# Moving the skip product, the rotations and one row-size pass in the second block of an S5 and Mish kernel

## The chip, the cores and the metric

The kernel runs on one core of one Trainium2 chip. The metric is the time of one execution on the device in microseconds (us). Of the kernel before there are three timed executions and one execution under the profiler.

The five engines have queues of their own. In the profile PE is the engine of the matmuls, PEld its weight loads, DVE the vector engine, ACT the scalar engine, POOL is GpSimd, and SP starts most of the DMAs. Instructions on one engine run in the order of its queue. An instruction that needs something from another engine waits on a semaphore, and everything behind it in the same queue waits with it.

## The reference: what is computed

From x (2048 x 1024) two branches are computed on the normalised rows xn = layernorm(x), and both are added to x:

```
xn  = layernorm(x)
Bu  = xn @ B_bar^T                        # complex, 1024 states
h_t = Lam_bar * h_(t-1) + Bu_t            # over 2048 steps
y   = 2 Re(h @ C^T) + xn * Dskip          # S5 branch, with the skip product
act = mish(xn @ w1 + b1)                  # 3584 columns
out = x + y + act @ w2
```

The part that the change touches most is the skip product xn * Dskip and its addition to x.

## The kernel before, in words

**Blocks.** The 2048 rows are done in four blocks of 512 (`blk` 0 to 3). The change concerns the second one, `blk == FAST == 1`; where the change in words says "block 2", this one is meant. A block lies in four row tiles of 128 (`q` 0 to 3): `xx` holds x, `xn` the normalised rows, `xnT` their transpose. Each block has a stage that projects into the states and into the Mish columns, a stage that multiplies the Mish columns by w2 (`tail`, line 1421: 28 column tiles by 8 output units), and a last one that multiplies the states by C (also line 1421, with hT).

**The order written out by hand.** In the second block the input projections are made by a form of Strassen's product with seven smaller products. `project_fast` walks through the string `WHOLE`, one token after another, and puts what the token stands for at the end of the queues:

- `a` to `d` with a number from 1 to 7: one of the seven products of a pair of state tiles (pair 0 to 3). `product` (line 935) issues 8 matmuls on PE, 128x256 each; `evacuate` then takes the sum out of PSUM.
- `p q s w` with a number: the same for a quad of Mish columns (`w_product`, line 1007, and `w_evacuate`, lines 1027 and 1044).
- `r` with a number: `rotate_in` of a state tile, three DVE instructions (lines 897, 903 and 905).
- `j` with a number: the skip product of a row tile.
- `T`: an ACT scaling of a rotation table. `k0`: one pending step that makes weight sums on DVE (line 1157) and stores them from POOL's queue (line 1136). `P`: weight sums on DVE (line 1669). `v`: a scaling of raw weights.
- `u` with a number: the first six column tiles of one output unit of the next stage. `g`: a Mish on ACT. `l`: loads of the next block's x, and `n`: loads of raw w1, both from POOL's queue.

**What an evacuation does.** A product leaves its sum in one of three PSUM banks X, Y and Z of its pair or quad. After product 1 and product 5, and after 6, ACT copies the bank to one of four buffers (`snaps`, line 952 for the pairs). After 1 for the pairs (2 for the quads), after 3 and after 7 DVE adds a bank and a copy into the result: a join (line 960 for the pairs, line 1044 for the quads). The copy buffer and the bank come free when the join has run.

The banks are shared over time. Pair c has X, Y, Z = 4, 5, 6 and pair d has 0, 1, 2. Quad s has 7, 5, 6 and quad w has 3, 1, 2. So s5 writes bank 6, which the join after c3 has to free, w5 writes bank 2 (join after d3), and c4 writes bank 4 (join after c7).

**The skip product.** `skip_slow` (lines 601 to 606) does it on POOL for the second block: a product into `xn` in place, and an addition to `xx`. The other blocks use `ln_skip` (lines 592 to 600), which does the same two steps on DVE with `mt` for the product.

**The statistics of the next block.** After `project_fast`, `next_stats` (lines 575 to 579) makes sums of the next block's rows on ACT, and `w_abs(0)` (line 1092) sizes the raw weights of quad 0 on ACT, one pass over 128x4096. The loop over the eight state tiles follows: `recur` (lines 1383, 897, 1390, 1392) on DVE for each. At tile 1 `next_root` (ACT line 583, DVE lines 585 and 586) and `next_scale` (ACT, line 590) stand in it, then `w_abs(1)`, `w_abs(2)` and `w_row(1)`. What they size is used in `w_exponent(1)` after the last tile. The normalised rows of the next block go through `transpose_dma` in SP's queue.

**Loads.** SP fills a ring of seven slots (lines 444 and 447). The load of a slot stands behind a wait until PE has used up what was in it.

Of the kernel before, what the change touches and what calls it, by code (L numbers as in the profile page):

```python
# [5 lines left out]
ALU = mybir.AluOpType  # L6
# [157 lines left out]
def build_kernel(nc, A_x, A_Lambda_re, A_Lambda_im, A_B_re, A_B_im, A_C_re, A_C_im,  # L164
# [18 lines left out]
    SPLIT = range(2, NB)  # L183
    GROUPS = ((0, 7), (7, NPL), (NPL, NPL + 8), (NPL + 8, NF), (12, 16), (16, 20), (20, 24), (24, 28))
    TILES = [*range(12)]
    WHOLE = ("a2 a1 b2 b1 a5 b5 P4 P5 a6 b6 v6 P6 P7 a3 b3 P0 a7 b7 P1 j0 p1 q1 a4 b4 "
# [3 lines left out]
    STEPS = ("p1 p5 p2 q1 q5 k0 k0 p6 q2 s1 k0 p7 s5 p3 k0 q6 s2 k0 p4 q7 k0 q3 k0 s6 q4 k0 m3 k0 g0 a2 a1 k0 s7 s3 k0 b2 b1 k0 s4 g1 m2 l0 a5 "  # L190
            "b5 a6 b6 a3 b3 a7 b7 c2 d2 a4 b4 c5 c1 d5 d1 h12 r0 c6 c3 h13 d6 d3 h14 c7 h15 w1 d7 r1 w5 w2 c4 d4 w6 x1 x5 x2 k0 w7 k0 w3 r2 "
            "x6 w4 y1 y5 y2 k0 x7 k0 x3 y6 A0 x4 z1 z5 g2 h8 h9 h10 M1 z2 y7 y3 z6 B0 h11 y4 z3 z7 u0 u2 r7 u1 z4 u7 r3 g3 r4 r6 r5")
# [20 lines left out]
    def sb(name, shape, dtype):  # L213
# [25 lines left out]
    xx = sb("xx", [P, 2, NQ, D], bf16)  # L239
    b_xx = [[Buf("xx%d_%d" % (i, q), parts=[Buf("xx%d_%d_%d" % (i, q, h)) for h in range(2)])  # L240
             for q in range(NQ)] for i in range(2)]
    s_xx = [[DmaSem(nc, "d_xx%d_%d" % (i, q)) for q in range(NQ)] for i in range(2)]
    xn = sb("xn", [P, NQ, D], bf16)
# [3 lines left out]
    dsk = sb("dsk", [P, D], bf16)  # L247
    b_dsk = Buf("dsk")
# [344 lines left out]
    def ln_skip(blk, q):  # L593

        i = blk % 2
        m = mt[:, q % 2, :, :].rearrange("p a t -> p (a t)")
        vop(lambda e: e.tensor_tensor(m, xn[:, q, :], dsk[:], op=ALU.mult),
            reads=[b_xn[q], b_dsk], writes=[b_m[q % 2]])
        vop(lambda e: e.tensor_tensor(xx[:, i, q, :], xx[:, i, q, :], m, op=ALU.add),
            reads=[b_xx[i][q], b_m[q % 2]], writes=[b_xx[i][q]])  # L600

    def skip_slow(blk, q):
        xb, b_x = xx[:, blk % 2, q, :], b_xx[blk % 2][q]
        pop(lambda e: e.tensor_tensor(xn[:, q, :], xn[:, q, :], dsk[:], op=ALU.mult),
            reads=[b_xn[q], b_dsk], writes=[b_xn[q]])
        pop(lambda e: e.tensor_tensor(xb, xb, xn[:, q, :], op=ALU.add), reads=[b_x, b_xn[q]], writes=[b_x])

    def transpose_dma(q):
        SP.dma(lambda e: e.dma_start_transpose(xnT[:, :, q * P:(q + 1) * P], xn[:, q, :]),
# [464 lines left out]
    def w_load(i):  # L1074
        sem = DmaSem(nc, "d_wraw%d" % i, nper=4)
        for ci in range(2):
            for kh in range(2):
                dst, b_dst = w_unit(w_raw(i, ci, kh))
                f0 = (4 * i + 2 * ci) * P
                src = B_w1[kh * NH * P:(kh + 1) * NH * P, f0:f0 + 2 * P].rearrange("(k p) f -> p k f", p=P)  # L1080
                PO.dma(lambda e, dst=dst, src=src: e.dma_start(dst.rearrange("p (k f) -> p k f", k=NH), src),
                       sem, writes=b_dst)
# [6 lines left out]
    def w_abs(i):  # L1089
        kind, t = w_raw(i, 0, 0)  # L1090
        v, b_v = (hb, b_hbf) if kind == "h" else (act, b_actf)
        aop(lambda e: e.activation(CT[:, :, 1, TB:D], v[:, t:t + 8, :], AF.Abs, accum_out=wsm(0, i, i + 1)),
            reads=b_v[t:t + 8], writes=b_snap + [b_wsm[0][i]])
# [211 lines left out]
    def project_fast(blk, order, open_unit):  # L1305
        keep = {}
        for o in order.split():
            kind, n = o[0], int(o[1:])
            if kind == "r":
                rotate_in(n)  # L1310
            elif kind == "u":
                open_unit(n)
            elif kind == "G":
                act_scale(n)
            elif kind == "g":
                mish(blk, n)
            elif kind == "k":
                if steps or later:
                    some(1)
                    ring_fill()  # L1320
            elif kind == "e":
                if later:
                    later.pop(0)()
            elif kind in "mMht":
                {"m": d2_load, "h": d2_row, "t": act_sums, "M": lambda n: d2_load(n, AC)}[kind](n)
            elif kind in "AB":
                recur(blk, n, (kind,))
                done.append((blk, n))
            elif kind == "P":
                sums_B(3 - n // 4, (n % 4,))  # L1330
            elif kind == "f":
                scale_B(n)
            elif kind == "T":
                table_scale(n)
            elif kind == "j":
                skip_slow(blk, n)
            elif kind == "S":
                row_scales()
            elif kind == "I":
                for _ in range(n):  # L1340
                    item_done()
            elif kind == "l":
                for q in range(NQ):
                    load_x(PO, blk + 1, q)
            elif kind == "n":
                w_load(n)
            elif kind == "v":
                w_scale(n)
                w_sums(n, True)
            elif kind in QUADS:  # L1350
                w_product(blk, QUADS.index(kind), n)
                w_evacuate(blk, QUADS.index(kind), n, keep)
            else:
                product(blk, "abcd".index(kind), n)
                evacuate("abcd".index(kind), n, keep, kind in "ab" and blk != FAST)
        assert blk < NB - 1 or not (steps or later)
# [331 lines left out]
    for blk in range(NB):  # L1688
# [60 lines left out]
        if near and blk not in SPLIT:  # L1749
            for q in range(NQ):  # L1750
                next_stats(blk + 1, q)
            w_abs(0)
        if blk == NB - 1:
            next(out_stage)
        for j in range(NJ):
            if blk == 0 and j == NJ - 1:
                rows_scale(0)
                w_load(3)
                rows_fetch(0)
            if (blk, j) not in done:  # L1760
                recur(blk, j)
            if near and j == (4 if blk in SPLIT else 1):
                next_root()
                for q in range(NQ):
                    next_scale(blk + 1, q)
            if blk in SPLIT:
                if near and j == 0:
                    d2_scale(1)
                if near and j == 1:
                    next(out_stage)  # L1770
                    for g in range(4, 8):
                        row_sizes(blk, g)
                    next(out_stage)
                    d2_load(5)
                    some(4)
                    d2_load(0)
                    recur(blk, 2)
                    done.append((blk, 2))
                    row_powers(20, NF)
                    row_bound()  # L1780
                    d2_scale(5)
                    for q in range(NQ):
                        next_stats(blk + 1, q)
                if near and j == 2:
                    some(4)
                if near and j == 3:
                    recur(blk, 4, "A")
                    some(4)
                    recur(blk, 4, "B")
                    done.append((blk, 4))  # L1790
                    row_most()
                if near and j == 4:
                    for q in range(NQ):
                        transpose_dma(q)
                    d2_scale(0)
                if j == 6 and not near:
                    vop(lambda e: e.tensor_tensor(KS[:, 1, :, :], KS[:, 1, :, :], KS[:, 3, :, :], op=ALU.add),
                        reads=[b_KS[1], b_KS[3]], writes=[b_KS[1]])
                continue
            if blk:  # L1800
                if j == 1:
                    next(out_stage)
                    w_load(2)
                    w_abs(1)
                    w_abs(2)
                    w_row(1)
                if j == 7:
                    w_exponent(1)
                    row_powers(0, 20)
                    for i in (0, 1, 2):  # L1810
                        w_scale(i)
                continue
            if j == 0:
                ln_root()
                for q in range(NQ):
                    ln_scale(1, q)
                w_exponent(0)
            scale_C(j)
            if j:
                keep_C(j - 1)  # L1820
            if j < 4:
                next(out_stage)
            if j < 3:
                row_sizes(0, j + 7)
            if j == 3:
                for i in range(NHS):
                    rows_load(i)
            for i in {4: (0, 1, 2), 5: (3, 4, 5, 6), 6: (7, 8, 9, 10), 7: range(11, 16)}.get(j, ()):
                rows_size(i)
# [61 lines left out]
```

## Time and profile before

| what | us |
|---|---|
| median of three timed runs | 601.29 (600.86 to 601.71) |
| the profiled execution, its own time | 601.42 |
| its span, from the first to the last instruction | 600.2 |
| PE busy in the span | 588.9 |
| DVE, ACT, POOL busy | 500.1, 386.6, 179.3 |
| mean granted PE clock, as a share of full speed | 0.991 |

The span is 1.2 us shorter than the profiled execution's own time. The rows below are read so: "216.92 1.04 PE L1007 ... x8" is a row of the timeline, it begins 216.92 us after the span's start, lasts 1.04 us, is issued at line 1007 of the kernel and has eight instructions; a bracket behind it tells how long the engine was idle before it and whom it waited for. Matmul rows overlap, since a matmul's end lies behind the start of the next; the pace is read from start to start. In a row of the windows view, each engine's busy time stands in the order PE, PEld, DVE, ACT and POOL, then the granted PE clock, the busy share of the DMA engines, and GB/s.

### The profile page before, as it was taken

Reading aid. Unit: us, or ns where it says so; the run is one execution under the profiler, and the core shown is the slowest. Engines: PE = TensorE matmul, PEld = TensorE weight load, DVE = VectorE, ACT = ScalarE, POOL = GpSimd, SP = SyncE. Lnnn points to the kernel's source line nnn. Section 1 sums busy time; section 2 is a strip of 40 time slices with the busy share of each in tenths; the row PEclk is TensorE's granted clock in tenths of the full one; section 3 lists DMA queues with packets and bytes.
Section 4 is the critical chain, followed back from the end, with each engine's and each line's share of the span. In section 5 each row is a group of like instructions: output and inputs, shape, how many; then the busy total and the mean of one; then the engine's idle time right before and its main releaser. Section 6 shows DMA issues by size and latency. Waiting matters only on the chain.

```text
span 600.2 us, 9754 instructions
## 1 busy us (share of the span) xinstructions
PE 588.9 (98%) x3651; PEld 356.5 (59%) x3651; DVE 500.1 (83%) x722; ACT 386.6 (64%) x518; POOL 179.3 (30%) x233
## 2 busy tenths in 40 slices
PE   9999999999999959999999999999999999999998
PEld 7644444444448847544448888744445888854444
DVE  6998898999898898919956956999399578789996
ACT  4849985488588635896255656898450798893320
POOL 2899300223653690600121611135210023100000
PEclk9999999999999988999999999999999999999999
DMA  9999999996899565988698958999997966988831
GB/s 251 302 242 281 222 181 240 322 381 184 255 331 350 193 212 162 315 294 206 198 309 313 405 217 293 354 314 319 259 283 277 391 248 219 333 316 325 293 128 70
DMA packets 115993, 161.90 MB, mean 270 GB/s; under 512 B 56010, under 2 KB 67018, under 8 KB 115946
## 3 DMA queue, kind: packets, MB, share of 16 engines
q1 hardware_dynamic: 96768, 104.42, 57.9%
q0 software_dynamic: 14112, 46.28, 22.4%
q10 hardware_dynamic: 5066, 10.57, 4.8%
q8 instruction: 29, 0.48, 0.3%
q14 instruction: 18, 0.15, 0.1%
HBM read 115.09 MB, written 34.08 MB: 249 GB/s over the span
## 4 chain that ended last, share of the span: by engine, by line
PE 95%; DVE 2%; DMA 1%; issue 1%; ACT 1%; SPq 1%; DVEq 0%
PE ps L1421 42%; PE ps L1007 18%; PE ps L935 11%; PE ps L859 9%; PE ps L1478 7%; PE ps L1367 5%; DMA ring<-in_B_w_dram 1%; PE ps L678 1%; DVE mt L897 1%; PE ps L669 0%; DVE hT L905 0%; DVE hT L903 0%; DVE hT L960 0%; PE ps L1444 0%; ACT act L1027 0%
## 5 line engine op out<-in xcount | busy, mean ns | idle before, releaser
L1421 PE MATMUL ps<-ring,act 128*128 128x512 bf16 x672 | 145.9, 379 | 0.0
L1421 PEld LDWEIGHTS ps<-ring,act 128*128 128x128 bf16 x672 | 65.7, 98 | 78.4
L1027 ACT ACTIVATE snaps<-ps,par,cs 128x256 f32<-128x256 f32 x98 | 53.6, 563 | 59.0 <-PE ps L1007 42.7
L1421 PE MATMUL ps<-ring,hT 128*128 128x512 bf16 x370 | 80.3, 379 | 0.0
L1007 PE MATMUL ps<-TT,ring 128*128 128x256 f16 x576 | 72.1, 275 | 7.6 <-DVE hT L960 7.6
L897 DVE TENSOR_TENSOR mt<-hT,tab 128x2048 bf16<-128x2048 bf16 (+1 forms) x56 | 71.2, 1272 | 1.3
L1007 PEld LDWEIGHTS ps<-TT,ring 128*128 128x128 f16 (+1 forms) x576 | 56.5, 98 | 15.7 <-DVE hT L960 7.9
L1184 POOL DMA_DIRECT2D w2d<-hb x42 | 30.0, 715 | 117.1 <-DVE hb L1212 71.0
L1421 PEld LDWEIGHTS ps<-ring,hT 128*128 128x128 bf16 x370 | 36.2, 98 | 43.6
L1383 DVE TENSOR_TENSOR_SCAN hT<-cs,qi,hT 128x512 bf16<-128x512 f32 x48 | 58.9, 1267 | 0.0
L1044 DVE SCALAR_TENSOR_TENSOR act<-ps,cs,snaps 128x512 bf16<-128x512 f32 x54 | 39.9, 748 | 21.2 <-PE ps L1007 19.4
L859 PE MATMUL ps<-xnT,ring 128*128 128x512 bf16 x264 | 57.3, 379 | 0.0
L1007 PE MATMUL ps<-xnT,ring 128*128 128x256 bf16 x432 | 54.6, 273 | 0.0
L1007 PEld LDWEIGHTS ps<-xnT,ring 128*128 128x128 bf16 (+1 forms) x432 | 42.4, 98 | 5.5
L859 PEld LDWEIGHTS ps<-xnT,ring 128*128 128x128 bf16 x264 | 25.8, 98 | 30.9
L882 ACT ACTIVATE act<-act 128x2048 bf16<-128x2048 bf16 (+3 forms) x12 | 32.8, 2756 | 6.8 <-DVE act L1030 6.8
L1136 POOL DMA_DIRECT2D wsd<-hb x35 | 19.0, 544 | 58.9 <-DVE hb L1157 31.0
L960 DVE TENSOR_TENSOR hT<-ps,snaps 128x512 f16<-128x512 f32 x36 | 23.9, 686 | 12.8 <-ACT snaps L952 10.4
L1142 ACT ACTIVATE hb<-hb,cs 128x2048 bf16<-128x2048 bf16 x10 | 19.4, 1994 | 22.4 <-DVE cs L1131 15.9
L867 ACT ACTIVATE act<-ps,par 128x512 bf16<-128x512 f32 (+1 forms) x40 | 23.9, 655 | 10.6 <-PE ps L859 10.5
L1367 PE MATMUL ps<-xnT,BT 128*128 128x512 bf16 x128 | 27.8, 379 | 0.0
L1421 PE MATMUL ps<-CT,hT 128*128 128x512 bf16 x128 | 27.8, 379 | 0.0
(226 smaller groups left out, 1014.4 us busy)
## 6 DMA issues: line engine op xcount, KB each, us to landing
ring<-wsd SPq DMA_DIRECT2D x126, 256.0 KB, 5.4
ring<-in_B_w_dram SPq DMA_DIRECT2D x62, 512.0 KB, 5.7
ring<-ctd SPq DMA_DIRECT2D x24, 512.0 KB, 4.4
ring<-w2d SPq DMA_DIRECT2D x24, 512.0 KB, 5.2
w2d<-hb POOLq DMA_DIRECT2D x42, 256.0 KB, 5.2
wsd<-hb POOLq DMA_DIRECT2D x35, 256.0 KB, 5.0
hb<-in_B_w_dram POOLq DMA_DIRECT2D x20, 256.0 KB, 5.9
ctd<-CT ACTq DMA_DIRECT2D x8, 512.0 KB, 5.8
```

The source lines that it names most:

```text
L859: PE.mm(lambda e, k=k, w=w: e.matmul(ps[:, bank, :], lhsT=w, rhs=xnT[:, k, :], start=k == 0, stop=k == NK - 1), reads=[b_ring[s]] + b_xnT, ...
L882: aop(lambda e: e.activation(t, t, AF.Mish), reads=b, writes=b)
L897: vop(lambda e: e.tensor_tensor(mt[:], u.unsqueeze(1).to_broadcast([P, 2, 2, TB]), tab[:, :, j, :].unsqueeze(2).to_broadcast([P, 2, 2, TB] ...
L935: PE.mm(lambda e, w=w, x=x, o=o, begin=begin, end=end: e.matmul(ps[:, bank, o:o + TH], lhsT=w, rhs=x, start=opens and begin, stop=end, ski ...
L1007: PE.mm(lambda e, w=w, x=x, o=o, begin=begin, end=end: e.matmul(ps[:, bank, o:o + TH], lhsT=w, rhs=x, start=opens and begin, stop=end, ski ...
L1027: aop(lambda e, o=o, p=p, j=j: e.activation(o, p, AF.Identity, scale=ig, bias=b1(f0 + j)), reads=[b_ps[b], b_par, b_ig], writes=b_dst)
L1044: vop(lambda e: e.scalar_tensor_tensor(out=dst, in0=bank(b), scalar=ig, in1=src, op0=ALU.mult, op1=ALU.add), reads=[b_ps[b], b_snap[k], b_ ...
L1184: PO.dma(lambda e: e.dma_start(w2d[at // 4][:, at % 4 * TB:(at % 4 + 2) * TB].rearrange("p (j t) -> p j t", j=2), t[:, :, d, :]), sem, rea ...
L1367: PE.mm(lambda e, j=j, ci=ci, k=k, bank=bank: e.matmul(ps[:, bank + ci, :], lhsT=BT[:, ci, j, k, :], rhs=xnT[:, k, :], start=k == 0, stop= ...
L1383: vop(lambda e, ci=ci, init=init: e.tensor_tensor_scan(out=hT[:, ci, j, :], data0=cj("r", j).to_broadcast([P, TB]), data1=hT[:, ci, j, :], ...
L1421: PE.mm(lambda e: e.matmul(ps[:, u, :], lhsT=lhsT, rhs=rhs, start=st_, stop=last, skip_group_check=blk == NB - 1), reads=reads, writes=[b_ ...
L1478: PE.mm(lambda e: e.matmul(ps[:, bank, :], lhsT=lhsT, rhs=rhs, start=st_, stop=end, skip_group_check=True), reads=[b_t, b_ring[s]], writes ...
```

## The change

Three things are changed, all in the second block:

1. `j0` to `j3` call `ln_skip` (DVE) and no longer `skip_slow` (POOL), which goes away. `j0` moves from a place before p1 to one behind d1, `j1` and `j2` from before c1 and before c5 to one behind T6, `j3` from before c7 to one behind d7.
2. All eight rotations move back in the order. Before, r0 stood behind d1, r1 behind T6 and r2 behind d7. Now r0 stands behind d4, r1 behind w2, r2 behind w7, r3 behind w4, and r4 to r7 in the last pieces. The order of the products is the same.
3. `w_abs(0)` moves from behind `next_stats` to behind `next_scale` and `w_load(2)`.

```diff
-    WHOLE = ("a2 a1 b2 b1 a5 b5 P4 P5 a6 b6 v6 P6 P7 a3 b3 P0 a7 b7 P1 j0 p1 q1 a4 b4 "
+    WHOLE = ("a2 a1 b2 b1 a5 b5 P4 P5 a6 b6 v6 P6 P7 a3 b3 P0 a7 b7 P1 p1 q1 a4 b4 "
              "k0 k0 p5 q5 k0 p2 q2 k0 p6 q6 P2 T4 p3 P3 q3 p7 q7 k0 c2 d2 p4 q4 T5 "
-             "k0 k0 k0 j1 c1 d1 r0 j2 c5 d5 T6 r1 c6 d6 T7 c3 d3 j3 c7 d7 r2 s1 s5 c4 d4 "
-             "r3 w1 w5 s2 w2 s6 w6 r4 s3 w3 s7 w7 u4 s4 w4 r5 u5 l0 u6 u7 n0 g4 g5 n1 r6 g6 g7 r7")
+             "k0 k0 k0 c1 d1 j0 c5 d5 T6 j1 j2 c6 d6 T7 c3 d3 c7 d7 j3 s1 s5 c4 d4 r0 "
+             "w1 w5 s2 w2 r1 s6 w6 s3 w3 s7 w7 r2 u4 s4 w4 r3 u5 l0 u6 u7 n0 g4 r4 g5 n1 r5 g6 r6 g7 r7")
...
-    def skip_slow(blk, q):
-        xb, b_x = xx[:, blk % 2, q, :], b_xx[blk % 2][q]
-        pop(lambda e: e.tensor_tensor(xn[:, q, :], xn[:, q, :], dsk[:], op=ALU.mult),
-            reads=[b_xn[q], b_dsk], writes=[b_xn[q]])
-        pop(lambda e: e.tensor_tensor(xb, xb, xn[:, q, :], op=ALU.add), reads=[b_x, b_xn[q]], writes=[b_x])
...
             elif kind == "j":
-                skip_slow(blk, n)
+                ln_skip(blk, n)
...
                 next_stats(blk + 1, q)
-            w_abs(0)
...
                     w_load(2)
+                    w_abs(0)
                     w_abs(1)
                     w_abs(2)
                     w_row(1)
```

## The prediction

> **What bounds the kernel now.** I read the page's busy shares first, then the table of who waited for whom, then the windows and the timeline where it pointed.
>
> ```profile
> PE 588.9 (98%) x3651; PEld 356.5 (59%) x3651; DVE 500.1 (83%) x722; ACT 386.6 (64%) x518; POOL 179.3 (30%) x233
> PE ps L1007 <- DVE hT L960: 7.6, 1, 7.6
> ```
>
> PE is busy nearly throughout, so the kernel gets faster only where PE stands still or runs slowly. In the table of waits one wait of PE is longer than 1.0 us: a single one of 7.6 us for a join of DVE (L960). The windows show where, and what it costs beyond itself (PE's busy time is the third number, the granted clock stands after the bracketed counts).
>
> ```profile
> 215.00:220.00 5.00, 2.96 (x28) 2.41 (x25) 4.96 (x3) 0.77 (x1) 4.86 (x3) 1.00 0.90 328
> 220.00:225.00 5.00, 0.00 (x0) 0.00 (x0) 4.97 (x4) 0.00 (x0) 4.17 (x2) 0.57 0.01 2
> 225.00:230.00 5.00, 4.41 (x21) 3.15 (x22) 4.93 (x8) 2.84 (x5) 0.00 (x0) 0.50 0.27 72
> ```
>
> From 220 to 225 PE does nothing while DVE and POOL are full, and from 225 to 230 PE works at a granted clock of 0.50. PE's timeline gives the price.
>
> ```profile
> 216.92 1.04 PE L1007 MATMUL ps<-xnT,ring 128*128 128x256 bf16 x8
> 225.59 1.89 PE L1007 MATMUL ps<-TT,ring 128*128 128x256 f16 x8 [7.63 <-DVE hT L960]
> ...
> 230.68 1.15 PE L1007 MATMUL ps<-xnT,ring 128*128 128x256 bf16 x8
> 231.67 1.04 PE L1007 MATMUL ps<-TT,ring 128*128 128x256 f16 x8
> 232.54 1.91 PE L1007 MATMUL ps<-xnT,ring 128*128 128x256 bf16 x16
> ```
>
> In the order of the tokens the first row is s1, the second s5, then c4 and d4, then w1 (230.68), w5 (231.67) and s2. At full clock a product takes 0.87 us, from 231.67 to 232.54. From the start of s1 to that of w5 lie five products, 4.37 us at 0.874 each; they took 231.67 - 216.92 = 14.75 us. **The stop costs 10.38 us**: 7.63 of waiting, 24 matmuls in 5.09 us instead of 2.62 (2.47), and 0.28 at the edges.
>
> Why the join is late is seen where DVE and POOL stand side by side.
>
> ```profile
> 205.57 2.86 DVE L1157 TENSOR_TENSOR hb<-hb 128x1024 f16<-128x1024 bf16 x4
> 211.35 1.29 DVE L960 TENSOR_TENSOR hT<-ps,snaps 128x512 f16<-128x512 f32 x2 [2.92 <-ACT snaps L952]
> 212.56 2.21 DVE L897 TENSOR_TENSOR mt<-hT,tab 128x2048 bf16<-128x2048 f16 x1
> 214.80 2.22 DVE L903 TENSOR_TENSOR hT<-mt 128x512 bf16<-128x512 bf16 x1
> 216.95 2.34 DVE L905 TENSOR_TENSOR hT<-mt 128x512 bf16<-128x512 bf16 x1
> 219.32 3.02 DVE L897 TENSOR_TENSOR mt<-hT,tab 128x2048 bf16<-128x2048 f16 x1
> 222.38 2.22 DVE L903 TENSOR_TENSOR hT<-mt 128x512 bf16<-128x512 bf16 x1
> ...
> 224.85 2.47 DVE L960 TENSOR_TENSOR hT<-ps,snaps 128x512 f16<-128x512 f32 x4
> 227.25 1.21 DVE L897 TENSOR_TENSOR mt<-hT,tab 128x2048 bf16<-128x2048 f16 x1
> ...
> 229.29 1.23 DVE L897 TENSOR_TENSOR mt<-hT,tab 128x2048 bf16<-128x2048 f16 x1
> ...
> 246.43 2.46 DVE L1383 TENSOR_TENSOR_SCAN hT<-cs,qi,hT 128x512 bf16<-128x512 f32 x2
> ```
>
> ```profile
> 208.72 0.54 POOL L1136 DMA_DIRECT2D wsd<-hb  x1 [0.18 <-issue]
> 209.28 2.14 POOL L604 TENSOR_TENSOR xn<-xn,dsk 128x1024 bf16<-128x1024 bf16 x1
> ...
> 213.64 3.11 POOL L604 TENSOR_TENSOR xn<-xn,dsk 128x1024 bf16<-128x1024 bf16 x1
> 216.89 2.12 POOL L606 TENSOR_TENSOR xx<-xx,xn 128x1024 bf16<-128x1024 bf16 x1
> ...
> 221.41 2.91 POOL L606 TENSOR_TENSOR xx<-xx,xn 128x1024 bf16<-128x1024 bf16 x1
> ```
>
> Behind the joins of c1 and d1 come r0 and r1, and only then the joins of c3, d3, c7 and d7 (the four at 224.85). A rotation takes 2.04 us when POOL is quiet, from 227.25 to 229.29 (r2). r0 and r1 ran while POOL multiplied and added, and took 212.56 to 224.85 = 12.29 us, 8.2 more than two quiet ones. Their ends follow POOL's: POOL's rows end at 216.75, 219.01 and 224.32, and the next DVE instruction ends at 217.02, 219.29 and just before 224.85. So each DVE instruction with two SBUF operands waits for a POOL instruction. s5 needs the bank that the join of c3 frees. That join ended at 224.85 + 0.69, and PE went on at 225.59.
>
> **The change part by part.**
>
> *Skip products on DVE.* POOL loses eight instructions, and nothing on POOL then computes in this stretch; its last DMA issue before it is at 208.72. DVE gains eight. Their price is to be seen in the third block's rows, and a locked one in the first block, beside POOL.
>
> ```profile
> 297.45 0.69 DVE L597 TENSOR_TENSOR mt<-xn,dsk 128x1024 bf16<-128x1024 bf16 x1
> ...
> 303.05 0.68 DVE L1676 TENSOR_TENSOR TT<-xnT 128x1024 f16<-128x1024 bf16 x1
> ```
>
> ```profile
> 29.69 1.76 DVE L597 TENSOR_TENSOR mt<-xn,dsk 128x1024 bf16<-128x1024 bf16 x1
> 31.48 1.06 DVE L599 TENSOR_TENSOR xx<-xx,mt 128x1024 bf16<-128x1024 bf16 x1
> ```
>
> Four skips run from 297.45 to 303.05, so an instruction takes 5.60 / 8 = 0.70 us. The locked pair averages 1.41. I take 0.70: the locked pair ran beside computing POOL rows, which are gone here, and beside POOL's DMA issues the four DVE instructions at 205.57 took 0.72 each. Below 0.70 nothing speaks for a gain.
>
> *The order on DVE.* The joins of c1 and d1 waited for ACT's copies (the bracket at 211.35), and what ACT and PE do before is unchanged, so DVE is free at 212.56 as before. Then j0, j1, j2: 6 x 0.70 = 4.20, to 216.76. The four joins took 224.85 to 227.25, 0.60 each: c3 ends at 217.36, d3 at 217.96, c7 at 218.56, d7 at 219.16, each 0.09 later counting the last one's full 0.69. PE would like to start s5 at 216.92 + 0.87 = 217.79 (bank freed at 217.45: no wait), c4 at 218.67 (218.65: just in time), d4 at 219.54 (219.25). With the 0.05 from a join's end to PE (225.54 to 225.59), c4 waits some 0.03. So the 10.38 us go, all but 0.1 at most; each 0.1 us by which a skip instruction is longer adds 0.6 behind it.
>
> What is late next? j3 takes 219.16 to 220.56. Behind it r0 stands where r3 stood and r1 about where r4 stood, at 2.04 each, so the joins of s and w have no more ahead of them than before, when PE did not wait for them. r2 comes behind the join of w7, and r3 to r7 when only the open units are left to PE. With PE's rows moved 10.38 earlier, w7's join ends near 230.0, and six rotations last until 242.3. The first `recur` began at 246.43 before, so even DVE's long chain starts 4 us earlier.
>
> *The size pass behind the scaling.* It costs no work, only order.
>
> ```profile
> 261.52 1.28 ACT L1092 ACT_TABLE_LOAD   x1
> 262.81 3.62 ACT L1092 ACTIVATE CT<-hb 128x4096 bf16<-128x4096 bf16 x1
> 268.17 0.18 DVE L585 RECIPROCAL ln<-ln 128x4 f32<-128x4 f32 x1 [12.80 <-ACT ln L583]
> 306.33 0.17 DVE L1408 TENSOR_TENSOR qi<-qi,qt 128x8 f32<-128x8 f32 x1
> 317.25 1.04 PE L1007 MATMUL ps<-xnT,ring 128*128 128x256 bf16 x8
> ```
>
> DVE waited 12.80 us for the root, behind a pass of 1.28 + 3.62 + 0.19 = 5.1 us on ACT. The pass goes behind `next_scale`, so the wait shrinks to some 2 us (DVE's wait began at 255.37 and begins 4 earlier, at 251.2; ACT's statistics end 10.4 earlier than 261.52, at 251.1, and a table load of 1.28 and the root follow). DVE goes on near 253 and no longer at 268.17, so its last work before the third block would end near 306.3 - 15 = 291, and PE's block near 317.25 - 10.4 = 306.9. Before, the cover was 317.25 - 306.33 = 10.9 us, after it some 15. This edit is worth nothing in the time, since PE and not DVE sets the end; without the cover it would be a gain of up to 12.80 - 2 = 10.8 us, not a loss. `w_row(1)` isn't delayed, since ACT does the same work before the third pass ends.
>
> *The queues.* The skips issue no DMA, and POOL's waits are shorter, not longer. SP's ring waits for PE, so its loads move with PE.
>
> ```profile
> 201.44 14.17 SPq L444 DMA_DIRECT2D ring<-wsd  x13
> 232.78 2.11 SPq L447 DMA_DIRECT2D ring<-in_B_w_dram  x2
> DMA to landing us min/median/max: 3.3/5.1/5.3
> 239.53 1.46 PE L1421 MATMUL ps<-ring,act 128*128 128x512 bf16 x6
> ```
>
> The thirteen loads of s and w weights were issued by 201.44 + 14.17 = 215.6. With the 5.3 of the w2 loads taken for them too, an estimate, the last has landed by 221; PE wants w1, which is early among them, at 220.4 and the last, s4, at 230.4. The third w2 load goes out at 234.5, lands 5.3 later at the longest (the third row is for five of these loads), at 239.8, and is wanted at 239.53 + 0.87 = 240.4. All three move with PE, so 0.6 us of margin stay.
>
> **Sum.** 601.42 - 10.38 + 0.05 = 591.09 for the profiled execution. That execution stands 0.13 above the median of the runs, less than their spread, so I give **591.1 us**.
>
> [...]
>
> **The rivals.**
>
> *A shorter stop stays.* Some joins still come late, by a skip instruction that is longer than 0.70, or by a copy of ACT that a join needs. For it: c4 has no slack. Against it: no row of a quiet POOL shows more than 0.72. At 0.80 the stop is 0.6 us. In the trace the half clock came some 2.8 us after PE's stop at 217.96 (the windows' 0.57 between 220 and 225), so a stop below that costs itself alone: 591.8 to 593.9.
>
> *The time saved is lost downstream.* PE comes 10.4 us earlier to the third w2 load, which is late: the pause no longer lets the DMA engines empty (busy share 0.01 between 220 and 225). For it: 0.6 us of margin. Against it: the load is bound to PE, and to lose all it has to take 5.3 + 0.6 + 10.4 = 16 us against a longest of 5.3. Then 601, no change; half of it gives 596.
>
> [...]
>
> **How the numbers follow.** Forecast (590.4 to 591.8): 0.80. Shorter stop (591.8 to 593.9): 0.10. Lost downstream: 0.07, of which 0.03 end within 0.2% of before and 0.04 near 596. Slower: 0.03. The range goes from 590.4 (the sum less 0.56, by which the fastest run lies under the profiled execution, rounded down) to 593.9, the end of the first rival; it holds 0.9 of the cases before any doubt about them. About 0.2% (1.2 us) can be told from no change here: faster 0.94, same 0.03, slower 0.03.
>
> **What would show it.** In the table of waits PE's 7.6 us for L960 is gone; no window of the second block has a PE clock below 0.9; PE goes from s1 to w5 in 4.4 us; lines 597 and 599 show four more instructions each near 0.69; the rotations all take 2.0; DVE's wait at L585 is near 2 us. I am wrong if skip rows near 215 last over 1 us, if PE waits for DVE before c4, or if PE stops at the first open unit (239.53 before, 229.15 after) for a load.

## The result, and the profile after

The changed kernel takes 591.11 us (median of five runs, 590.79 to 591.26), against 601.29 us before (five runs, 600.86 to 601.71). The ratio is 0.983, with a 95% interval of 0.9816 to 0.9844. The forecast was 591.1. The profiled execution took 591.11 us, with a span of 589.9 us.

The change takes out six lines ahead of the places of interest, so line numbers fall by 6: the joins of the pairs are at L954 (L960 before), the rotations at L891, L897 and L899, the products at L929 and L1001.

PE's first line on the page and its whole table of waits are now these (the table's columns: who waited for whom, total us, times, longest us):

```profile
PE 586.5 (99%) x3651; PEld 355.8 (60%) x3651; DVE 494.2 (84%) x730; ACT 384.6 (65%) x517; POOL 159.9 (27%) x225
PE ps L625 <- DVE filler L457: 1.0, 1, 1.0
PE ps L663 <- DMA ring<-in_B_w_dram: 0.2, 1, 0.2
```

The wait of 7.6 us is gone, and what is left lies in the first 12 us of the span. The windows of the same stretch as before:

```profile
215.00:220.00 5.00, 5.00 (x49) 4.48 (x47) 4.93 (x9) 2.69 (x5) 0.00 (x0) 1.00 0.94 337
220.00:225.00 5.00, 5.00 (x49) 4.48 (x46) 3.96 (x7) 3.45 (x7) 0.54 (x1) 1.00 0.57 193
225.00:230.00 5.00, 5.00 (x45) 4.21 (x43) 4.60 (x7) 2.15 (x4) 0.82 (x2) 1.00 0.97 341
```

PE is busy for all 15 us, at a clock of 1.00, beside a DVE that is nearly as full as before. The timeline shows the order in which DVE now works, and PE beside it:

```profile
211.45 1.29 DVE L954 TENSOR_TENSOR hT<-ps,snaps 128x512 f16<-128x512 f32 x2 [2.92 <-ACT snaps L946]
212.66 0.68 DVE L597 TENSOR_TENSOR mt<-xn,dsk 128x1024 bf16<-128x1024 bf16 x1
...
216.03 0.69 DVE L599 TENSOR_TENSOR xx<-xx,mt 128x1024 bf16<-128x1024 bf16 x1
216.64 2.48 DVE L954 TENSOR_TENSOR hT<-ps,snaps 128x512 f16<-128x512 f32 x4
...
220.48 1.23 DVE L891 TENSOR_TENSOR mt<-hT,tab 128x2048 bf16<-128x2048 f16 x1
```

```profile
217.03 1.04 PE L1001 MATMUL ps<-xnT,ring 128*128 128x256 bf16 x8
217.90 1.04 PE L1001 MATMUL ps<-TT,ring 128*128 128x256 f16 x8
218.78 1.91 PE L929 MATMUL ps<-TT,BT 128*128 128x256 f16 x16
...
221.40 1.04 PE L1001 MATMUL ps<-TT,ring 128*128 128x256 f16 x8
```

The three skip products run from 212.66 to 216.64, 3.98 us and so 0.66 an instruction, and the four joins follow at once. From the start of s1 (217.03) to that of w5 (221.40) PE takes 4.37 us, the time of five products at full clock: the 10.38 us are gone to the last tenth. This measure, s1 to w5 less 4.37, is called the *loss of the stretch* from here on.

Further on, DVE has more room than before:

```profile
242.32 2.46 DVE L1377 TENSOR_TENSOR_SCAN hT<-cs,qi,hT 128x512 bf16<-128x512 f32 x2
252.87 0.18 DVE L585 RECIPROCAL ln<-ln 128x4 f32<-128x4 f32 x1 [1.61 <-ACT ln L583]
...
281.09 0.67 DVE L1120 TENSOR_REDUCE cs<-wmx 128x3 f32<-128x384 f32 x1 [1.30 <-DMA wmx<-wmd]
292.43 0.17 DVE L1402 TENSOR_TENSOR qi<-qi,qt 128x8 f32<-128x8 f32 x1
306.98 1.04 PE L1001 MATMUL ps<-xnT,ring 128*128 128x256 bf16 x8
```

The first scan begins at 242.32 (before 246.43), the wait for the root is 1.61 us (12.80), and DVE's last row begins 14.55 us before PE begins the third block (10.92). PE's block ends 10.27 us earlier, and the span is 10.3 us shorter: nothing was lost on the way to the end.

### The profile page after: what moved, and what is told of

It is laid out like the page before. It is cut to its first block, busy times and chain, and to the rows that moved or that the text cites. A ratio compares the mean times of both kernels' runs of the same rounds, so it can differ in the third digit from the quotient of the medians.

```text
span 589.9 us, 9744 instructions
## 1 busy us (share of the span) xinstructions
PE 586.5 (99%) x3651; PEld 355.8 (60%) x3651; DVE 494.2 (84%) x730; ACT 384.6 (65%) x517; POOL 159.9 (27%) x225
## 4 chain that ended last, share of the span: by engine, by line
PE 98%; DMA 1%; SPq 1%; DVE 0%; issue 0%
PE ps L1415 43%; PE ps L1001 19%; PE ps L929 12%; PE ps L853 10%; PE ps L1472 7%; PE ps L1361 5%; DMA ring<-in_B_w_dram 1%; PE ps L672 1%; PE ps L663 0%; PE ps L1438 0%; SPq L397 0%; PE ps L1446 0%; PE ps L505 0%; SPq L447 0%; SPq L401 0%; DVE xx L1572 0%
## 5 line engine op out<-in xcount | busy, mean ns | idle before, releaser
L1001 PE MATMUL ps<-TT,ring 128*128 128x256 f16 x576 | 71.2, 273 | 0.0
L891 DVE TENSOR_TENSOR mt<-hT,tab 128x2048 bf16<-128x2048 bf16 (+1 forms) x56 | 68.5, 1223 | 1.4
L1001 PEld LDWEIGHTS ps<-TT,ring 128*128 128x128 f16 (+1 forms) x576 | 56.2, 98 | 7.5 <-issue 0.2
L1001 PE MATMUL ps<-xnT,ring 128*128 128x256 bf16 x432 | 54.5, 273 | 0.0
L1001 PEld LDWEIGHTS ps<-xnT,ring 128*128 128x128 bf16 (+1 forms) x432 | 42.3, 98 | 5.3
L954 DVE TENSOR_TENSOR hT<-ps,snaps 128x512 f16<-128x512 f32 x36 | 23.9, 688 | 12.5 <-ACT snaps L946 10.2
```

The lines of the kernel that those rows point to most:

```text
L891: vop(lambda e: e.tensor_tensor(mt[:], u.unsqueeze(1).to_broadcast([P, 2, 2, TB]), tab[:, :, j, :].unsqueeze(2).to_broadcast([P, 2, 2, TB] ...
L1001: PE.mm(lambda e, w=w, x=x, o=o, begin=begin, end=end: e.matmul(ps[:, bank, o:o + TH], lhsT=w, rhs=x, start=opens and begin, stop=end, ski ...
```

## The experiments

The theory is that of the prediction: POOL's computing instructions hold up DVE's instructions with two SBUF operands (r0 and r1 took 12.29 us, two quiet rotations 4.08), a join waits for whatever stands ahead of it on DVE, PE waits for the join (7.63 us), and a long stop of PE halves its clock for a while (0.50 from 225 to 230). The rivals were that only one of the three edits matters, that the lock lies elsewhere, and that the clock follows another rule. Each kernel was compared with the kernel before on the same chip, whose median was 601.47 us beside e1 to e4, 601.72 beside e5 to e8, and 601.22 beside e9 to e12.

### One edit alone: e1, e2, e3

e1, on the kernel before: the skip product on DVE, all tokens where they were.

```diff
             elif kind == "j":
-                skip_slow(blk, n)
+                ln_skip(blk, n)
```

> The skip products go to DVE in their old places; rotations and size pass stay as before. Theory (only a computing POOL holds DVE up, and the joins come after whatever stands ahead of them): behind the joins of c1 and d1 DVE does r0, j2 and r1 in 2.04 + 1.4 + 2.04 us, c3's join ends near 218.7 and c7's, behind j3, near 221.3. s5 waits about 1.0 us and c4 1.7, no half clock: 593.7. Rival (without POOL's lock the order of the rotations does not matter): 591.1. Rival (the work on DVE costs what the lock did): 601.

e2: the eight `r` tokens where the change has them, everything else as before.

```diff
-             "k0 k0 k0 j1 c1 d1 r0 j2 c5 d5 T6 r1 c6 d6 T7 c3 d3 j3 c7 d7 r2 s1 s5 c4 d4 "
-             "r3 w1 w5 s2 w2 s6 w6 r4 s3 w3 s7 w7 u4 s4 w4 r5 u5 l0 u6 u7 n0 g4 g5 n1 r6 g6 g7 r7")
+             "k0 k0 k0 j1 c1 d1 j2 c5 d5 T6 c6 d6 T7 c3 d3 j3 c7 d7 s1 s5 c4 d4 r0 "
+             "w1 w5 s2 w2 r1 s6 w6 s3 w3 s7 w7 r2 u4 s4 w4 r3 u5 l0 u6 u7 n0 g4 r4 g5 n1 r5 g6 r6 g7 r7")
```

> The rotations alone move; the skip products stay on POOL in their old places. Theory (the lock holds DVE's instructions with two SBUF operands; a join reads one operand from PSUM and is not held): the joins run at 0.6 to 0.7 us beside POOL, s5 does not wait, r0 is stretched to some 6 us without PE waiting long for s2's join: 591.1 to 592.0. Rival (POOL holds the joins too): three joins of 2.2 us each, c7's join 5 us later, 595 to 598. Rival (the skip must leave POOL for any gain): 601.

e3: `w_abs(0)` behind the scaling, as in the change, and nothing else.

```diff
                 next_stats(blk + 1, q)
-            w_abs(0)
...
                     w_load(2)
+                    w_abs(0)
```

> The size pass of quad 0 alone moves behind the scaling. Theory: DVE's wait for the root falls from 12.8 us to near 8 or less and the time stays at 601.3, since PE sets the end and DVE has 10.9 us of cover. Rival (DVE's chain counts): 596 or less.

Measured: e1 595.55 us (ratio 0.990, 0.9881 to 0.9919), e2 592.43 (0.9842, 0.9823 to 0.9861), e3 601.43 (1.0006, 0.9991 to 1.0021).

PE's timeline of e1 has the two stops that were worked out, before s5 and before c4:

```profile
218.93 1.04 PE L1007 MATMUL ps<-xnT,ring 128*128 128x256 bf16 x8
220.73 1.05 PE L1007 MATMUL ps<-TT,ring 128*128 128x256 f16 x8 [0.77 <-DVE hT L960]
223.25 1.92 PE L935 MATMUL ps<-TT,BT 128*128 128x256 f16 x16 [1.48 <-DVE hT L960]
...
225.88 1.04 PE L1007 MATMUL ps<-TT,ring 128*128 128x256 f16 x8
```

From 218.93 to 225.88 are 6.95 us, so the loss of the stretch is 2.58 against the 2.7 expected. e1's span is 594.4, 4.5 above that of the changed kernel; the rest stands before the stretch, where s1 begins at 218.93 and not at 217.03. There is a wait of 1.42 us near 185, which has its own section below. In its clock this profile is not typical: its mean granted clock is 1.000, while the other three timed runs of e1 have 0.997, so some time at half clock, which the expectation had excluded. What the half clock costs is worked out with e5 and e10.

e2 is the sharpest of the three. In its timeline the joins run while POOL computes, and only the rotation behind them is stretched:

```profile
216.05 0.69 DVE L960 TENSOR_TENSOR hT<-ps,snaps 128x512 f16<-128x512 f32 x1 [1.87 <-PE ps L935]
...
218.67 0.69 DVE L960 TENSOR_TENSOR hT<-ps,snaps 128x512 f16<-128x512 f32 x1 [0.18 <-PE ps L935]
219.28 1.38 DVE L897 TENSOR_TENSOR mt<-hT,tab 128x2048 bf16<-128x2048 f16 x1
220.69 2.23 DVE L903 TENSOR_TENSOR hT<-mt 128x512 bf16<-128x512 bf16 x1
222.84 2.33 DVE L905 TENSOR_TENSOR hT<-mt 128x512 bf16<-128x512 bf16 x1
```

```profile
217.45 2.12 POOL L606 TENSOR_TENSOR xx<-xx,xn 128x1024 bf16<-128x1024 bf16 x1
219.53 3.10 POOL L604 TENSOR_TENSOR xn<-xn,dsk 128x1024 bf16<-128x1024 bf16 x1
222.78 2.12 POOL L606 TENSOR_TENSOR xx<-xx,xn 128x1024 bf16<-128x1024 bf16 x1
```

A join has one operand in PSUM and takes 0.69 us beside POOL; an addition of 128x512 with both operands in SBUF takes 2.2 to 2.3 instead of 0.42, its time in the kernel before when POOL had stopped:

```profile
228.49 0.42 DVE L903 TENSOR_TENSOR hT<-mt 128x512 bf16<-128x512 bf16 x1
```

PE's stretch is at full speed: s1 at 218.47, w5 at 222.84, 4.37 us. So moving the rotations alone takes away the whole stop. The time of 592.43 lies a little above the 592.0 that was expected at most, and e2's span 1.4 above that of the changed kernel; its wait near 185 is 1.39 us.

e3 moves DVE's wait for the root from 12.8 to 7.8 us and the time not at all, as cover of 10.9 us has it.

### The lock without the order: e4, e7, e8

e4, on the kernel before: the `j` tokens do nothing, so this kernel leaves out the skip product of the second block.

```diff
             elif kind == "j":
-                skip_slow(blk, n)
+                pass
```

> The order of before without the skip products of the second block: xn * Dskip is left out for its 512 rows. Theory (the lock alone makes the joins late): r0 and r1 take 2.04 us each, c3's join ends near 217.4 and c7's near 218.6, PE does not wait: 591.1, as after the change. Rival (two rotations ahead of the joins are too much in any case): PE still waits over 1 us, 592.3 or more.

e7, on the changed kernel: six stores of `xx` from POOL's queue behind j0.

```diff
                 ln_skip(blk, n)
+                if n == 0:
+                    for m in range(6):
+                        PO.dma(lambda e, m=m: e.dma_start(xtra[m], xx[:, blk % 2, 0, :]), s_nat[m],
+                               reads=[b_xx[blk % 2][0]])
```

> The changed kernel with six further DMA issues of 128x1024 on POOL's queue, behind j0, stores of xx into unused DRAM, so that they run beside j1, j2 and the joins. Theory (DMA issues of POOL do not hold DVE): lines 597 and 599 stay at 0.69 us, 591.1 to 591.5. Rival (they hold DVE as computing instructions do): instructions of 1 us or more beside them, PE waits, 594 or more.

e8, on the changed kernel: six products on POOL behind j0.

```diff
                 ln_skip(blk, n)
+                if n == 0:
+                    for _ in range(6):
+                        pop(lambda e: e.tensor_tensor(xn[:, 0, :], xn[:, 0, :], dsk[:], op=ALU.mult),
+                            reads=[b_xn[0], b_dsk], writes=[b_xn[0]])
```

> The changed kernel with six products of 128x1024 on POOL, in place on xn of row tile 0 after j0 has read it (the tile is not read any more), beside j0 to j2 and the joins. Theory (each DVE instruction with two SBUF operands waits for a POOL instruction of some 2.2 us): j0's addition, j1 and j2 end near 224.6, c3's join near 225.3, PE stops 7.4 us and runs at half clock after it: 601.4, about the time of before the change. Rival (the skip's instructions on DVE are not held): 591.1.

Measured: e4 591.31 us (0.9827, 0.9805 to 0.9849), e7 591.5 (0.9831, 0.9804 to 0.9859), e8 600.19 (0.9967, 0.9947 to 0.9987).

e4 has the old order with two rotations ahead of the joins and loses nothing in the stretch (s1 at 217.03, w5 at 221.40). Together with e2 this settles what made the stop: two rotations *and* the lock. Without either of the two the joins are in time.

In e7, whose lines stand one further on, the six issues lie at 214.90 to 218.12, beside skip products that keep their price:

```profile
214.52 0.68 DVE L598 TENSOR_TENSOR mt<-xn,dsk 128x1024 bf16<-128x1024 bf16 x1
215.24 0.69 DVE L600 TENSOR_TENSOR xx<-xx,mt 128x1024 bf16<-128x1024 bf16 x1
```

```profile
214.90 3.22 POOL L1334 DMA_DIRECT2D xtra<-xx  x6 [4.99 <-DVE xx L600]
```

In e8 POOL computes instead, and each instruction of j1 and j2 is held (lines 597 and 599 take 0.68 and 0.69 us in the changed kernel):

```profile
214.52 2.61 DVE L597 TENSOR_TENSOR mt<-xn,dsk 128x1024 bf16<-128x1024 bf16 x1
217.17 2.49 DVE L599 TENSOR_TENSOR xx<-xx,mt 128x1024 bf16<-128x1024 bf16 x1
...
224.63 2.47 DVE L954 TENSOR_TENSOR hT<-ps,snaps 128x512 f16<-128x512 f32 x4
```

The joins begin at 224.63, as late as before the change (224.85), PE stops for 6.76 us, and the loss of the stretch is 8.89 us (s1 at 217.57, w5 at 230.83). The stop was to be 7.4 us and the time 601.4; s1 itself began 0.65 us later than before the change. With the change's own order, the lock brings nearly the old time back.

### How a stop is paid: e5, e6, e11, e12

These put N further products (N = 4, 8, 2, 3) on DVE behind j2 in the changed kernel, so that the joins come later and PE stops for a length that was chosen.

```diff
                 ln_skip(blk, n)
+                if n == 2:
+                    for _ in range(4):
+                        vop(lambda e: e.tensor_tensor(mt[:, 0, :, :].rearrange("p a t -> p (a t)"), xn[:, 2, :], dsk[:],
+                                                      op=ALU.mult), reads=[b_xn[2], b_dsk], writes=[b_m[0]])
```

> The changed kernel with four further DVE products (128x1024, two SBUF operands, the result thrown away) behind j2, so that the joins of c3 to d7 come 2.9 us later. Theory (a short stop costs itself; PE has about 0.2 us of slack before c4): 2.7 us more than the changed kernel, 593.8, no half clock. Rival (cost in proportion to before, 10.38 us for 7.63 of waiting, 1.36 each): 594.8.

> The changed kernel with eight such products behind j2: the joins come 5.8 us later, PE stops for over 5 us. Theory (half clock from about 2.8 us after the stop until about 5 us after the restart, 2.6 us lost): 5.5 + 2.6 = 8.1 more, 599.2. [...] Rival (no half clock below 7 us of stop): 596.6.

> The changed kernel with two further DVE products behind j2: PE stops some 0.8 us before s5 and 0.3 before c4. Theory (a stop of 1.5 us or less, as the two in e1, brings no half clock): 1.25 us above e9 and a clock of 1.00 throughout. Rival (any stop costs about 1.75 times its length, as the 2.4 us of e5 cost 4.2): 2.2 above e9.

> The changed kernel with three further DVE products behind j2: PE stops some 1.5 us before s5 and 0.3 before c4. Theory (the half clock needs a stop between 1.5 and 2.2 us): 1.97 us above e9 and a clock of 1.00. Rival (the half clock comes for this one already and costs about 1.8 us more): 3.8 above e9.

| kernel | N | time, ratio to before | PE's wait before s5 | loss of the stretch | expected |
|---|---|---|---|---|---|
| e11 | 2 | 593.29, 0.9866 (0.9837 to 0.9896) | 0.76 | 1.26 | 1.25 |
| e12 | 3 | 593.12, 0.9864 (0.9839 to 0.9890) | 1.49 | 1.98 | 1.97 |
| e5 | 4 | 595.57, 0.9893 (0.9869 to 0.9917) | 2.22 | 4.17 | 2.7 |
| e6 | 8 | 598.90, 0.9949 (0.9919 to 0.9979) | 5.13 | 7.28 | 8.1 |

For N = 2 and 3 the order on DVE gives the loss to a hundredth, at a clock of 1.00. In both the loss has a second, smaller part: c4 and d4 begin 0.33 us late as well. The time of e11 stands 2.20 us above e9, which is the number of its rival; the stretch and the clock decide against the rival, and the rest is very likely the wait near 185, 1.61 us in e11's profile and absent from that of e12. For N = 4 the theory fell: a stop of 2.22 us brought a half clock, which began only after PE had gone on.

```profile
217.55 1.04 PE L1001 MATMUL ps<-xnT,ring 128*128 128x256 bf16 x8
220.81 1.16 PE L1001 MATMUL ps<-TT,ring 128*128 128x256 f16 x8 [2.22 <-DVE hT L954]
222.01 3.37 PE L929 MATMUL ps<-TT,BT 128*128 128x256 f16 x16
```

c4 and d4 take 3.37 us and not 1.91. What rule the clock follows is read from the two windows of 1 us in which it changes: a window wholly inside the slow phase shows 0.50 (225 to 230 before the change), so a granted clock of c means that a share 2c - 1 of that us went at full speed. For e5, e6, e8 and the kernel before, in this order:

```profile
221.00:222.00 1.00, 0.97 (x8) 0.52 (x6) 1.00 (x3) 0.97 (x2) 0.00 (x0) 0.80 0.08 31
225.00:226.00 1.00, 1.00 (x11) 0.90 (x10) 0.89 (x3) 0.58 (x1) 0.00 (x0) 0.99 0.00 0
```

```profile
221.00:222.00 1.00, 0.00 (x0) 0.00 (x0) 0.96 (x2) 0.00 (x0) 0.00 (x0) 0.90 0.45 172
228.00:229.00 1.00, 1.00 (x8) 0.78 (x7) 0.97 (x2) 0.59 (x1) 0.00 (x0) 0.69 0.93 354
```

```profile
222.00:223.00 1.00, 0.00 (x0) 0.00 (x0) 0.97 (x2) 0.00 (x0) 1.00 (x1) 0.80 0.00 0
229.00:230.00 1.00, 1.00 (x9) 0.82 (x8) 0.97 (x2) 0.58 (x1) 0.00 (x0) 0.79 1.02 397
```

```profile
220.00:221.00 1.00, 0.00 (x0) 0.00 (x0) 1.00 (x1) 0.00 (x0) 1.00 (x1) 0.83 0.03 10
230.00:231.00 1.00, 1.00 (x7) 0.71 (x5) 0.97 (x3) 0.08 (x1) 0.00 (x0) 0.55 0.43 164
```

In e5 the half clock lasts from 221.60 to 225.02, 3.42 us; in e6 from 221.80 to 228.62 and in e8 from 222.60 to 229.42, 6.82 us; before the change from 220.66 to 230.90, 10.24 us. These are one, two, two and three times 3.41 us, the mean of the eight steps (27.30 / 8). An estimate from these lengths is a clock that changes in whole steps of 3.41 us, so that what a stop costs beside itself depends on how it falls into the steps.

The mean clocks of the timed runs count the steps as well: one step at half clock takes 3.41 / 2 = 1.7 us out of some 600, 0.003 of the mean. All four runs of e5 have 0.997. Of e6's nine, seven have 0.994 (two steps), one 0.997 and one 0.991. Of the 44 runs of the kernel before beside the experiments, 21 have 0.994 and 23 have 0.992 or less, so it has two steps in some executions and three or more in others.

For e6 the theory's price of the slow phase, 2.6 us, missed: PE was at work in it from 224.53 to 228.62, so half of 4.09, 2.0 us, was lost, and the loss of the stretch is 7.28 and not 8.1. The rival without a half clock missed too: the clock was 0.50 after a stop of 5.13 us, and the time is 598.90 and not 596.6.

### Chance, and a wait ahead of the change: e9 and e10

e9 is the changed kernel and e10 the kernel of e1, both once more.

> The changed kernel once more, as the measure for the three beside it. In five of the runs so far PE waited 0.6 to 1.4 us near 185, ahead of everything that the change moves, for DVE's scaling of B, which stood behind a weight sum that waited for a store to land; in the changed kernel's first profile it did not. Theory (that wait is chance in the DMAs' timing): 591.1 to 592.5, with or without it. Rival (it belongs to the other kernels alone): 591.1 and no wait near 185.

> The kernel of e1 once more: skip products on DVE in their old places. Theory (its two stops cost 2.6 us and the rest of e1's 4.5 us was the wait near 185): 593.7 if PE does not wait near 185, and up to 595.5 if it does; the time from the start of s1 to that of w5 is 6.95 us again, against 4.37. Rival (the skip product before p1 delays something else): more than 2.6 us above e9 with no wait near 185.

Measured: e9 591.09 us (0.983, 0.9805 to 0.9855), e10 595.25 (0.9906, 0.9879 to 0.9933).

e10 has the same two stops as e1 and no wait near 185, yet its stretch takes 8.62 us and not 6.95:

```profile
216.64 1.04 PE L1007 MATMUL ps<-xnT,ring 128*128 128x256 bf16 x8
218.44 1.05 PE L1007 MATMUL ps<-TT,ring 128*128 128x256 f16 x8 [0.77 <-DVE hT L960]
220.97 3.25 PE L935 MATMUL ps<-TT,BT 128*128 128x256 f16 x16 [1.48 <-DVE hT L960]
...
225.26 1.04 PE L1007 MATMUL ps<-TT,ring 128*128 128x256 f16 x8
```

```profile
221.00:222.00 1.00, 1.00 (x7) 0.78 (x8) 1.00 (x2) 0.00 (x0) 0.00 (x0) 0.69 0.89 330
224.00:225.00 1.00, 1.00 (x7) 0.75 (x6) 0.97 (x2) 0.59 (x1) 0.00 (x0) 0.61 0.00 0
```

The second fence is of the two windows with a change of clock: half from 221.38 to 224.78, 3.40 us, one step. PE's first stop ended at 218.44, so 0.47 us of it lie in the 3.41 us before 221.38, and all of the second: 1.95 us of standing still in that step. In the profile of e1 the same two stops brought no half clock. The same kernel pays 2.58 or 4.25 us for the same stops. Of e10's ten timed runs six have a mean clock of 1.000, three 0.997 and one 0.994. That is a part of its spread, 593.86 to 600.4 us, against 590.92 to 591.12 for four runs of e9; it isn't all of it, since the six at 1.000 alone go from 593.86 to 598.11, which stays unexplained. With its time of 595.25 and a further wait of 1.1 us elsewhere, e10 doesn't give the 593.7 that was expected without a wait near 185; its fastest run, 593.86, is near it. The number of the rival came in (more than 2.6 us above e9, with no wait near 185), but not for the reason that the rival gave: s1 begins at 216.64, no later than in the changed kernel, so the skip product before p1 delays nothing, and the loss is that of the two stops, the half clock and the further wait.

The wait near 185 can be followed to its source, though not to why it varies. ACT scales raw weights as soon as their load has landed, and behind the scaling it evacuates the Mish column tiles 8 to 11; b2 on PE then needs the bank of tile 9, the second of the four. In e11:

```profile
179.87 3.89 ACT L1136 ACTIVATE act<-act,cs 128x2048 bf16<-128x2048 bf16 x2 [4.23 <-DMA act<-in_B_w_dram]
183.67 2.40 ACT L861 ACTIVATE act<-ps,par 128x512 bf16<-128x512 f32 x4
185.06 1.91 PE L929 MATMUL ps<-xnT,BT 128*128 128x256 bf16 x16 [1.61 <-ACT act L861]
```

PE went on at 185.06, 1.39 us after the evacuations began. In all seven profiles with this wait the two lie 1.38 or 1.39 us apart, also in e1 and e8, where PE's row names DVE. And the wait of PE follows the wait of the scaling for its load:

| ACT's wait for the load, us | PE's wait near 185, us | profiles |
|---|---|---|
| 1.16 to 2.66 | none | before and after the change, e3, e4, e7, e10, e12 |
| 2.90 | 0.16 | e9 |
| 3.31 | 0.57 | e5, e6 |
| 3.54 | 0.80 | e8 |
| 4.13, 4.15 | 1.39, 1.42 | e2, e1 |
| 4.23 | 1.61 | e11 |

So the expectation of e9 named the wrong engine, and its rival fell too: e1 and e10 are one kernel, with the wait and without it, and e9 had 0.16 us of it where the changed kernel's first profile had none. The wait is therefore not fixed by the kernel: the same kernel has it in one execution and not in another. What makes the load land late is not shown. The changed kernel's nine timed runs, 590.79 to 591.26, show next to none of it.

## Why the prediction was right, point by point

- **The price of the stop, 10.38 us.** It came from five products between two starts of PE's timeline. The span fell by 10.3, the time by 10.2. It is the price of one execution, with three slow steps; other executions of the same kernel had two. The sum did not suffer, since it starts from the time of the same execution.
- **The price of a skip product on DVE, 0.70 us an instruction.** It was 0.66 to the start of the next. The locked row of 1.41 was rightly left out: e7 shows that POOL's DMA issues hold nothing up (0.68 and 0.69 beside six of them), e8 that computing POOL would have (2.5 to 2.6).
- **The order on DVE.** c3's join was given for 217.36 to 217.45 and PE's s5 without a wait; PE shows no wait from s1 to w5. e11 and e12, worked out by the same order, came within 0.01 us.
- **The edits of no worth.** The size pass gave 0 (e3), and DVE's cover grew to 14.55 us where some 15 were given. The wait for the root was 1.61 for "some 2", the first scan 242.32 for 242.3. A new wait came with it that I had denied: DVE now reaches `w_exponent` 1.30 us before its data (L1120). The cover hides it.
- **The queues.** PE never waited for w2 at the first open unit.
- **What was wrong, in a rival.** "A stop below that costs itself alone", with 2.8 us as the bound, fell with e5 (a stop of 2.22 us) and e10 (0.77 and 1.48). With it falls the fixed price of 2.6 us that I gave e6 and e8: their half clock was two steps, that of before three. The end of the range at 593.9 rested on that bound; a rest of a stop of 2.2 us would have given 595. (The other end was rounded too far down: 591.09 - 0.56 is 590.53, not 590.4. No run of the changed kernel came near it.)
- **What was incomplete.** I had the stop down to POOL's lock alone and listed the move of the rotations as a part of the order. Either would have done: the rotations alone (e2) or the absence of POOL's work (e4). The later rotations need no help from the skip products; it is the skip products that need the later places, since on DVE they take the room that the rotations had, and with the old order they leave two stops (e1).

## What to carry to other kernels

An engine that is nearly full is not the trouble as long as what others wait for stands early in its queue (from 215 to 220 DVE was busy for 4.93 us of 5 after the change, and PE waited for nothing); put work with a far due time behind the instruction that frees a bank, before making anything faster. Work on GpSimd was not free for VectorE here: beside its products those of j1 and j2 took 2.49 to 2.61 us and not 0.69 (e8), while a join beside them took 0.69 (e2). So look at which VectorE rows beside it grow, and which don't. A stop of TensorE is priced from a start before it to a start behind the slow phase, not by the row that names the wait (here 10.38 us against 7.63).

## What the runs showed of the hardware

The half clock came and went in steps of 3.41 us (3.40, 3.42, 6.82, 6.82 and 10.24 us long). For one step of it 2.22 us of standing still (e5), and 1.95 us in two pieces in the 3.41 us before it (e10), were enough.

A stop of 1.49 us, with a further 0.15 us before c4, was not (e12). Whether it was too short, or fell across two steps, is open: a trace without a half clock has no edge from which the steps could be counted. That the place in the step decides fits the one kernel that gave both 2.58 and 4.25 us of loss (e1 and e10).
